# A pre-LN block on one core: first gate and up weights prepared after block 5, LayerNorm rows of chunks 2 and 3 read a column group sooner

## The chip, the cores and the metric

The kernel runs on one NeuronCore of a Trainium2 chip. The metric is the time of one execution on the device, in microseconds (us). TensorE (PE in the profile) multiplies, VectorE (DVE), ScalarE (ACT) and GpSimd (POOL) work on the results, and SyncE (SP) issues most of the DMA transfers.

## The reference

One transformer block on x of 2048 rows and 640 columns, in fp32: sliding-window attention (32 heads of 20 columns, 256 keys back) behind a LayerNorm, then a gated feed-forward (640 to 1536 and back) behind another.

```python
def _A_ref(x, wqkv, wo):
    ...                       # q, k, v of 32 heads, Dh = 20, W = 256
    scores = jnp.einsum("bhqd,bhkd->bhqk", q, k) * (Dh ** -0.5)
    mask = (idx[:, None] - idx[None, :] >= 0) & (idx[:, None] - idx[None, :] < W)
    p = _softmax(jnp.where(mask[None, None], scores, -1e9), axis=-1)
    ...                       # o = p v, heads side by side
    return o @ wo

def _B_ref(x, w_gate, w_up, w_down):
    return (_gelu(x @ w_gate) * (x @ w_up)) @ w_down

h = x + _A_ref(_layernorm(x), wqkv, wo)
h2 = h + _B_ref(_layernorm(h), w_gate, w_up, w_down)
```

## The kernel before

**Number form.** Every fp32 factor is split into two fp16 halves, high and low, after scaling by a power of two. A product takes three matmuls: high by high, high by low, low by high. A weight passes through `Weight`: its raw rows are loaded, `scale` finds the largest magnitude on DVE (the tile `am`) and spreads it over the partitions with one small matmul, `split` writes the high half on ACT, and the low half is written on POOL (the first two pieces of the later weights) or DVE. In the profile the weights are w0 to w2 (q, k, v), w3 (output projection), w4 to w6 (gate, groups 0 to 2), w7 to w9 (up) and w10 to w12 (down); the halves of gate and up of group 0 lie in the tile `gu`. Their raw rows come in slices through a ring of three tiles, `wsl`, once for the maxima and once for the split. The gate, up and down weights behind them come one at a time through a single tile, `wst`.

**Attention.** The 2048 rows are 16 blocks of 128. For each block there are two passes over the scores: one for the row maxima (DVE, the tile `junk`), one for the exponentials (ACT, the tile `pt`). The values are accumulated in the PSUM bank `pv` and copied out by ACT into `oT`, twice per block. When the second half of block j has been copied, `B[j].scored` is set. The output projection adds to x in the tile `ht`, which is stored as rows of h in `h_dram`. `first_norm_lane` normalises blocks 0 to 3 of h from that tile, into a tile of its own, `lxn`, and transposes them with TensorE into `h0h` and `h0l`.

**Feed-forward.** The rows are four chunks of 512, the 1536 columns three groups of 512, each of four tiles (`ft`). `ORDER` lists the pairs (chunk, group). A group of gate and up columns is computed in one of two forms:

- `gate_up`, the plain form: for each tile 30 matmuls of 512 columns into two banks named `mm`. DVE's product of gate and up (the tile `gel`) releases the second.
- `quad`, the form with sums: sums and differences of the two halves of the chunk's rows (`token_sums`, the tiles `ts`) and of the weights (`weight_sums`, the tiles `ws`) replace part of the products. For each tile it takes ten matmuls of 512 columns and 35 of 256, into the banks `tp`, `ra`, `pv` and `rb`, and more additions on DVE and POOL (`quad_out`). The weight sums of a tile take two POOL and two DVE operations; they are stored in DRAM (`wsums`) and read back when a later chunk needs them.

`PLAIN` says how many of the pairs in `ORDER` are plain. In the plain pairs `down` of the pair before runs as a block behind the next one; in the others two of its eight groups of matmuls are laid behind each tile. `norm_start(c)` loads rows of h for chunks 1 to 3 into the ring `wsl`, and `norm_lane` normalises them on DVE and hands them to the DMA transpose on SP (`turned`). Chunk 2 reuses the tiles of chunk 0, and chunk 3 those of chunk 1, so that their transposes may only be issued when gate and up of the old chunk are through.

**Order of the work.** The program is written out by a planner. Each piece of work is a generator, a lane, which yields the engine that it needs next and the condition for it. `Clock` keeps a modelled time for each engine, and at each step the first lane in a list of priorities whose condition holds, and whose engine is not too far ahead (`FFBACK` and its kin), issues one instruction. The order on each engine is thus fixed when the program is built; on the chip each engine takes its instructions strictly in that order and waits for semaphores.

Of the kernel before, what the change touches and what calls it, by code (L numbers as in the profile page):

```python
# [22 lines left out]
P = 128  # L23
# [6 lines left out]
FG = 3  # L30
# [223 lines left out]
def block_kernel(ctx: ExitStack, tc: tile.TileContext, x, wqkv, wo, wg, wu, wd, out):  # L254
# [384 lines left out]
    def hpart(c, b):  # L639
        return tuple(t[:, :, b * P:(b + 1) * P] for t in hT[c])  # L640
# [419 lines left out]
    NCH = S // (CB * P)  # L1060
    ORDER = [(0, 0), (1, 0), (0, 1), (0, 2), (1, 1), (1, 2)]
    ORDER += [(c, fg) for c in range(2, NCH) for fg in range(FG)]
    PLAIN = 4
    hts, ga = {}, {}
    ffpools = [None, None]

# [197 lines left out]
    lnbuf = []  # L1264

    def norm_start(c):
        yield ("sync",), need(when=lambda: pos["gu", c - 2] == FG if c > 1 else (
            ffpools[0] and W["d", 0].ready and all(b.wrote for b in B[CB:2 * CB])), eng="sync")
        if c == 1:
            hT[1] = tuple(nc.tile(ffpools[0], [P, KC, CB * P], F16, n) for n in ("h1h", "h1l"))  # L1270
            lnbuf.extend(nc.tile(stage, [P, D], F32, "wsl", SLICES) for _ in range(3))
        else:
            hT[c] = hT[c - 2]
        for i, n in enumerate("hi"):
            side.append((LATE, norm_lane(c, (i, i + 2), n, lnbuf[i])))

    def norm_lane(c, bs, lane, t):
        for b in bs:
            j = c * CB + b
            yield ("sync",), lambda: nc.others(t, "sync")  # L1280
            nc.sync.dma_start(t, h_dram[j * P:(j + 1) * P, :])
            yield from layernorm(t, lane, *hpart(c, b), xn=lambda: t, dma=True)
            chunk[c] += 1
        if chunk[c] == CB:
            side.append((LATE, token_sums(c)))
# [3 lines left out]
    def token_sums(c):  # L1289
        hh, hl = hT[c]  # L1290
        h1, h2 = hh[:, :, :CW], hh[:, :, CW:]
        l1, l2 = hl[:, :, :CW], hl[:, :, CW:]
        yield on("vector", when=lambda: ffpools[1] and (c == 1 or W["d", FG - 1].ready))
        t = (nc.tile(ffp, [P, KC, 512], F32, "ts") if c % 2 else
             nc.tile(ffpools[0], [P, KC, 512], F32, "wst")).bitcast(F16)
        t = t.rearrange("p c (a n) -> p a c n", a=4)
        for ks in (slice(k, k + 1) for k in range(KC)):
            a, b, m, d = (t[:, i, ks] for i in range(4))
            yield on("vector", h1, h2)
            nc.vector.tensor_tensor(a, h2[:, ks], h1[:, ks], op=ALU.subtract)  # L1300
            yield on("vector", a, l2)
            nc.vector.scalar_tensor_tensor(b, a, -_pow2(-TE), l2[:, ks], op0=ALU.mult, op1=ALU.add)
            yield on("vector", b, l1)
            nc.vector.tensor_tensor(d, l1[:, ks], b, op=ALU.subtract)
            yield on("vector", l2, h2)
            nc.vector.scalar_tensor_tensor(m, l2[:, ks], _pow2(TE), h2[:, ks], op0=ALU.mult,
                                           op1=ALU.subtract)
        TS[c] = t

    WS = {}  # L1310
    QLOAD = [(c, fg) for c in range(2, NCH) for fg in range(FG) if (c, fg) != (2, 0)]
    wsums = dram.tile([FG * FT, P, 4 * KC * P], F16, name="wsums")

    def weight_sums(c, fg, ft):
# [23 lines left out]
    def first_norm_lane():  # L1338

        for b in range(CB):  # L1340
            yield on("vector", when=lambda: B[b].halves == 2)
            yield from layernorm(B[b].h, "h", *hpart(0, b),
                                 xn=lambda: nc.tile(lnp, [P, D], F32, "lxn"))
            B[b].normed = True
            chunk[0] += 1


    later = [(kind, fg) for fg in range(FG) for kind in "gud"]
# [13 lines left out]
    def scale_lane(todo, lane):  # L1362
        for i in todo:
            w = weights[i]
            before = {1: W["q"], 2: W["k"]}.get(i)
            yield on("vector", when=lambda: (w.loaded or w.sliced) and (not before or before.scaled)
                     and (i < NW or B[0].maxima == H) and (i <= NW or B[0].scored))
            yield from w.scale(lane, "ra" if i < NW else "tp")
            if i == 0:
                yield on("vector", sw)  # L1370
                nc.vector.tensor_scalar(qs, sw[:, C_Q:C_Q + 1], _pow2(QE), None, op0=ALU.mult)
                pos["qs"] = 1
            if i == 1:
                yield on("vector", when=lambda: W["q"].known)
                qk_scale()
            if i == NW:
                yield on("vector", when=lambda: W["v"].known)
                wo_scale()
            if i > NW:
                kind, fg = later[i - NW - 1]  # L1380
                if kind == "u":
                    ff_scales(fg)
                    pos["ffk", fg] = 1
                if kind == "d":
                    ff_scales_down(fg)
                    w.down = True
# [81 lines left out]
    def feed_forward():  # L1468
        quads = [(c, fg, ft) for c, fg in ORDER[PLAIN:] for ft in range(FT)]

        def sums_lane():
            for i, q in enumerate(quads):
                yield on("gpsimd", when=lambda: pos["quads"] >= i - 1 and W["d", 2].ready)
                yield from weight_sums(*q)

        side.append((LATE, sums_lane()))
# [167 lines left out]
```

## Time and profile before

| | us |
|---|---|
| median of 3 runs | 1042.01 |
| lowest and highest | 1041.12, 1042.12 |
| the profiled execution | 1043.35 |
| its span, first to last instruction | 1041.6 |

The span divides so: up to about 44 us loads, the first splits and projections; to about 605 us attention, with projections, output projection and feed-forward pair (0, 0) laid between; to 729 us the other plain pairs and their down projections; to the end the pairs with sums.

Times in the profile are us from the span's start, and a mean in a group is in ns. A row of the timeline has start, duration, engine, operation, `out<-in`, and in square brackets how long the engine had idled before and what ended that. "SPq" rows are the issues on SP's queue. All instructions carry line 199, since one helper issues them, so groups are told apart by the names of their tiles.

### The profile page before, as it was taken

How to read it: one execution, taken by the hardware profiler on the slowest of the kernel's cores; microseconds unless marked ns; L12 is line 12 of the kernel's file. 1: busy time of each engine (PE TensorE's matmuls, PEld its weight loads, DVE VectorE, ACT ScalarE, POOL GpSimd, SP SyncE). 2: the span in 40 equal slices, each digit the busy share in tenths (PEclk: the TensorE clock that was granted, in tenths of full speed). 3: DMA queues.
4: the chain of work that ended last, by engine and by line, in shares of the span. 5: the costliest groups of instructions: out<-in, count | busy, mean ns of one | idle time of the engine just before them, and what ended most of it. 6: DMA issues, size and time to landing. Idle time of an engine off the chain costs nothing.

```text
span 1041.6 us, 26895 instructions
## 1 busy us (share of the span) xinstructions
PE 1019.7 (98%) x10802; PEld 691.2 (66%) x10802; DVE 778.4 (75%) x2193; ACT 490.6 (47%) x938; POOL 269.8 (26%) x369
## 2 busy tenths in 40 slices
PE   8999999999999999999999899999999999999998
PEld 7876567667666666676655564555777777777776
DVE  6878989998787777677687867676997985445553
ACT  6512667666666766666667835341122222222220
POOL 7100332233333323232323511031445310000000
PEclk9999999999999999999999999999999999999999
DMA  8663354361341513415302341314342652122211
GB/s 300 149 133 114 119 121 132 122 150 55 73 107 43 101 45 77 77 44 112 129 28 90 78 139 52 101 51 127 102 144 110 164 166 77 59 94 102 77 51 51
DMA packets 89116, 105.86 MB, mean 102 GB/s; under 512 B 22176, under 2 KB 63392, under 8 KB 88992
## 3 DMA queue, kind: packets, MB, share of 16 engines
q1 hardware_dynamic: 76896, 93.41, 31.2%
q10 hardware_dynamic: 12096, 10.75, 3.2%
q8 instruction: 84, 1.38, 0.6%
q14 instruction: 40, 0.33, 0.1%
HBM read 71.11 MB, written 28.84 MB: 96 GB/s over the span
## 4 chain that ended last, share of the span: by engine, by line
PE 78%; DVE 13%; issue 3%; DMA 3%; ACT 2%; POOL 0%; SPq 0%; DVEq 0%; ACTq 0%
PE mm L199 40%; PE pv L199 11%; PE ra L199 11%; PE rb L199 9%; PE tp L199 7%; DVE junk L199 4%; DMA qT<-qk 1%; DVE am L199 1%; DMA wst<-in_wd_dram 1%; DVE m L199 1%; DVE al L199 0%; DVE ht L199 0%; ACT pt L199 0%; DVE qks L199 0%; DMA wsl<-h_dram 0%
## 5 line engine op out<-in xcount | busy, mean ns | idle before, releaser
L199 POOL TENSOR_SCALAR_AFFINE_SELECT pt<-pt 128x512 f32<-128x512 f32 x240 | 152.9, 659 | 361.4 <-ACT pt L199 358.7
L199 DVE CUSTOM_DVE_ANT_0 junk<-rb,mask 128x384 bf16<-128x384 f32 (+2 forms) x262 | 138.9, 530 | 42.4 <-PE rb L199 22.6
L199 DVE CUSTOM_DVE_ANT_0 junk<-ra,mask 128x384 bf16<-128x384 f32 (+2 forms) x250 | 132.2, 529 | 41.4 <-PE ra L199 22.3
L199 ACT ACTIVATE pt<-ra,esc 128x384 f32<-128x384 f32 (+2 forms) x248 | 130.7, 579 | 68.4 <-PE ra L199 57.3
L199 ACT ACTIVATE pt<-rb,esc 128x384 f32<-128x384 f32 (+2 forms) x232 | 122.0, 578 | 70.1 <-PE rb L199 59.2
L199 PE MATMUL pv<-pt,v 128*21 128x128 f32 x2880 | 104.8, 277 | 2.1 <-ACT oT L199 2.1
L199 PEld LDWEIGHTS <-ah 128*128 128x128 f16 x768 | 75.5, 98 | 31.1 <-issue 3.1
L199 ACT ACTIVATE gel<-gel,ffk 128x512 f32<-128x512 f32 x32 | 23.1, 722 | 121.4 <-DVE gel L199 121.4
L199 PEld LDWEIGHTS pv<-pt,v 128*21 128x21 f32 x2880 | 68.8, 101 | 17.0 <-ACT oT L199 2.8
L199 PEld LDWEIGHTS <-kT 62*128 62x128 f16 x1440 | 57.8, 95 | 22.7 <-issue 12.7
L199 PEld LDWEIGHTS <-ws 128*128 128x128 f16 x640 | 62.6, 98 | 7.2
L199 PEld LDWEIGHTS <-gu 128*128 128x128 f16 x440 | 42.1, 98 | 36.6 <-issue 1.5
L199 ACT CAST ah<-gel 128x512 f16<-128x512 f32 x48 | 29.6, 616 | 75.7 <-DVE gel L199 75.7
L199 DVE SCALAR_TENSOR_TENSOR ht<-mm,ffk,ht 128x320 f32<-128x320 f32 x96 | 51.9, 545 | 15.9 <-PE mm L199 13.8
L199 PEld LDWEIGHTS <-qT 60*128 60x128 f16 x640 | 24.5, 93 | 56.7 <-issue 55.3
L199 PE MATMUL mm<-xh,w1h 128*128 128x256 f16 x200 | 54.6, 273 | 1.6 <-DVE qks L199 1.6
L199 PE MATMUL mm<-xl,w1h 128*128 128x256 f16 x200 | 54.7, 273 | 0.0
L199 PE MATMUL mm<-xh,w1l 128*128 128x256 f16 x200 | 54.7, 273 | 0.0
L199 PE MATMUL mm<-w3h,oh 128*128 128x320 f16 x160 | 48.0, 300 | 0.1
L199 PE MATMUL mm<-w2h,xh 128*128 128x320 f16 x160 | 48.1, 300 | 0.0
L199 PE MATMUL mm<-w3l,oh 128*128 128x320 f16 x160 | 48.0, 300 | 0.0
L199 PE MATMUL mm<-w2h,xl 128*128 128x320 f16 x160 | 48.0, 300 | 0.0
(296 smaller groups left out, 2531.8 us busy)
## 6 DMA issues: line engine op xcount, KB each, us to landing
ws<-wsums SPq DMA_DIRECT2D x20, 640.0 KB
qk<-qks ACTq DMA_DIRECT2D x32, 256.0 KB
qT<-qk SPq DMA_DIRECT2D x48, 160.0 KB
kT<-qk SPq DMA_DIRECT2D x48, 160.0 KB
wsums<-ws SPq DMA_DIRECT2D x12, 640.0 KB
ht<-in_x_dram SPq DMA_DIRECT2D x16, 320.0 KB
h_dram<-ht SPq DMA_DIRECT2D x16, 320.0 KB
ht<-h_dram SPq DMA_DIRECT2D x16, 320.0 KB
```

Of the source, the lines that this page charges most:

```text
L199: r = real(*args, **kw)
```

## The change

- `PLAIN` goes from 4 to 3: the pair (0, 2) takes the form with sums, and the down projection of (0, 1) is laid between its matmuls.
- For this chunk 0 gets token sums too, in a tile of its own, `ts0`; the weight sums of a group are built as soon as its gate and up weights are split (before: once the last down weight was), and the rule for which pairs read stored sums is written in general form: those whose group has had sums before.
- `norm_start` for chunks 2 and 3 starts when two of the three groups of chunk c - 2 have been issued (before: all three). The condition on all three moves to the copy ahead of the transpose.
- `scale_lane` starts on the gate weight of group 0, and with it on all weights behind it, when block 5 is scored (before: block 0).
- `first_norm_lane` normalises in place, in `B[b].h`, and starts the token sums of chunk 0 when it is through.

```diff
-    PLAIN = 4
+    PLAIN = 3
...
     def norm_start(c):
-        yield ("sync",), need(when=lambda: pos["gu", c - 2] == FG if c > 1 else (
+        yield ("sync",), need(when=lambda: pos["gu", c - 2] == FG - 1 if c > 1 else (
             ffpools[0] and W["d", 0].ready and all(b.wrote for b in B[CB:2 * CB])), eng="sync")
...
-            yield from layernorm(t, lane, *hpart(c, b), xn=lambda: t, dma=True)
+            yield from layernorm(t, lane, *hpart(c, b), xn=lambda: t, dma=True,
+                                 when=lambda: c < 2 or pos["gu", c - 2] == FG)
...
-        yield on("vector", when=lambda: ffpools[1] and (c == 1 or W["d", FG - 1].ready))
-        t = (nc.tile(ffp, [P, KC, 512], F32, "ts") if c % 2 else
+        yield on("vector", when=lambda: ffpools[1] and (c < 2 or W["d", FG - 1].ready))
+        t = (nc.tile(ffp, [P, KC, 512], F32, "ts" if c else "ts0") if c % 2 or not c else
              nc.tile(ffpools[0], [P, KC, 512], F32, "wst")).bitcast(F16)
...
-    QLOAD = [(c, fg) for c in range(2, NCH) for fg in range(FG) if (c, fg) != (2, 0)]
+    QLOAD = [q for i, q in enumerate(ORDER) if q[1] in [fg for _, fg in ORDER[PLAIN:i]]]
...
             yield from layernorm(B[b].h, "h", *hpart(0, b),
-                                 xn=lambda: nc.tile(lnp, [P, D], F32, "lxn"))
+                                 xn=lambda: B[b].h)
             B[b].normed = True
             chunk[0] += 1
+        side.append((LATE, token_sums(0)))
...
-                     and (i < NW or B[0].maxima == H) and (i <= NW or B[0].scored))
+                     and (i < NW or B[0].maxima == H) and (i <= NW or B[5].scored))
...
-                yield on("gpsimd", when=lambda: pos["quads"] >= i - 1 and W["d", 2].ready)
+                yield on("gpsimd", when=lambda: pos["quads"] >= i - 1 and W["g", q[1]].ready
+                         and W["u", q[1]].ready)
```

## The prediction

> **What bounds the kernel now.** I read the page first, for who is busy; then the table of busy time by stage, with the cuts laid where the order of column groups changes; then the timeline of each engine at the one place where TensorE stands still, and last the groups by line for the prices.
>
> ```profile
> span 1041.6 us, 26895 instructions
> PE 1019.7 (98%) x10802; PEld 691.2 (66%) x10802; DVE 778.4 (75%) x2193; ACT 490.6 (47%) x938; POOL 269.8 (26%) x369
> ```
>
> TensorE is busy for 98% of the span, so only two things can shorten the run: fewer matmuls, or less of the 21.9 us in which it idles and of the time in which its clock is lowered. The stages show where those are (columns: stage, its length, busy time of PE, PEld, DVE, ACT and POOL, granted clock, DMA share, GB/s).
>
> ```profile
> 583.00:586.40 3.40, 1.55 (x31) 1.04 (x32) 2.51 (x4) 1.96 (x4) 1.67 (x2) 1.00 0.35 92
> ...
> 716.29:720.30 4.01, 4.01 (x18) 2.36 (x18) 2.86 (x7) 0.60 (x1) 0.41 (x1) 0.57 0.53 105
> ...
> 115.00:124.40 9.40, 7.66 (x98) 4.15 (x97) 8.82 (x29) 6.81 (x13) 2.44 (x3) 0.92 0.43 128
> 124.40:216.00 91.60, 88.64 (x1216) 59.69 (x1220) 84.98 (x290) 63.12 (x128) 29.61 (x47) 0.99 0.47 128
> ...
> 260.00:340.00 80.00, 79.09 (x1175) 53.91 (x1168) 62.56 (x211) 51.57 (x106) 25.49 (x42) 1.00 0.28 73
> 686.04:712.50 26.46, 26.39 (x124) 11.95 (x122) 17.38 (x25) 9.03 (x13) 9.34 (x6) 1.00 0.27 98
> 712.50:729.38 16.88, 14.88 (x98) 10.07 (x97) 12.82 (x35) 2.79 (x4) 1.65 (x3) 0.90 0.33 79
> 729.38:766.30 36.92, 36.92 (x278) 27.02 (x276) 35.09 (x64) 6.79 (x11) 14.89 (x12) 1.00 0.30 99
> 766.30:803.30 37.00, 37.00 (x279) 27.02 (x277) 30.79 (x55) 8.31 (x14) 17.83 (x13) 1.00 0.38 134
> ```
>
> The row from 686.04 is the plain gate and up of chunk 0, group 2; the row from 712.50 is the down projection of group 1 that stands alone behind it; the row from 729.38 is one whole column group in the form with sums, with eight down groups laid between its matmuls. In that last row TensorE has no gap although DVE is busy for 95%. In the row from 712.50 TensorE loses 2.00 us, and then runs 4.01 us at a clock of 0.57. The timeline names the cause, engine by engine.
>
> ```profile
> 702.68 5.02 SPq L199 DMA_DIRECT2D wsums<-ws  x2
> 705.95 1.40 POOL L199 TENSOR_TENSOR ws<-w5h,ws 128x640 f16<-128x640 f16 x1 [1.36 <-DVE ws L199]
> 707.74 1.38 SPq L199 DMA_DIRECT2D wsl<-h_dram  x2
> 711.95 0.89 DVE L199 BATCH_NORM_STATS2 lsth<-wsl 128x6 f32<-128x320 f32 x2 [3.52 <-DMA wsl<-h_dram]
> 715.50 0.73 DVE L199 SCALAR_TENSOR_TENSOR gel<-mm,ffk,gel 128x512 f32<-128x512 f32 x1
> 715.97 1.23 SPq L199 DMA_TRANSPOSE h0h<-wsl  x1
> 716.29 0.30 PE L199 MATMUL mm<-w11h,ah 128*128 128x320 f16 x1 [2.00 <-DVE gel L199]
> ```
>
> Read it from the bottom. TensorE waits for an mm bank, which the last gelu product (DVE, 715.50) releases. That product stands in DVE's queue behind the row statistics of chunk 2, which waited 3.52 us for rows of h. Those loads were issued at 707.74, because SP had spent 5.02 us on two stores of weight sums, the second of which waited for POOL (705.95 + 1.40 = 707.35).
>
> **The change, part by part.** *Group (0, 2) in the form with sums (PLAIN 3).* The two rows 26.46 + 16.88 = 43.34 us become one stage like the next one, 36.92 us: **-6.4 us**. Of this 2.00 us are the wait, (1 - 0.57) x 4.01 = 1.7 us the lowered clock, and the other 2.7 us fewer matmuls (seven of 256 columns and two of 512 for each k tile in place of six of 512) plus the scale step of the last down weight, whose small matmul stands in the first row; I take 0.5 us of that back, since it only moves: **-5.9 us**.
>
> *Rows of chunks 2 and 3 read a group sooner.* The reads, two rows at first, are then issued when gate and up of (0, 1) have been issued, ahead of the sum stores in SP's queue instead of behind them. Behind the statistics DVE still has the last gelu product of (0, 1) and the accumulations of down (1, 0), and TensorE waits for their mm banks: this is the same configuration at 672. Nothing in SP's queue waits for POOL there, so the rows come 711.95 - 707.74 = 4.2 us after issue, about as the schedule plans them. Cost nothing; if that cover fails, the old 2.0 + 1.7 us return. The transposes now wait for the end of (0, 2); what needs them, chunk 2's first quad, comes two groups later (74 us), and each takes 1.23 us on SP (715.97).
>
> *The first quad needs its weight sums.* This is the added wait.
>
> ```profile
> 680.88 1.40 DVE L199 SCALAR_TENSOR_TENSOR w9l<-wst,sw,w9h 128x512 f16<-128x512 f32 x2
> 686.04 0.38 PE L199 MATMUL mm<-h0h,w6h 128*128 128x512 f16 x1
> 696.38 1.84 POOL L199 TENSOR_TENSOR ws<-w5l,w8l 128x640 f16<-128x640 f16 x1
> 701.25 1.40 POOL L199 TENSOR_TENSOR ws<-w5h,ws 128x640 f16<-128x640 f16 x1 [3.03 <-DVE ws L199]
> 702.61 1.98 POOL L199 TENSOR_TENSOR ws<-w5l,w8l 128x640 f16<-128x640 f16 x1
> ```
>
> The up weight of group 2 (w9) is split by 682.28. A set of sums took 701.25 + 1.40 - 696.38 = 6.3 us the first time and 707.35 - 702.61 = 4.7 us the second: ready at 687.0 to 688.6. TensorE arrives at 686.04, needs the first sum after ten small matmuls and the last one later, so the wait is 0 to about 2 us. All that TensorE does later stands behind it. Later sets have 9.2 us each (36.92 / 4).
>
> *Token sums of chunk 0.* Twenty more DVE operations between the end of attention (605) and 686.
>
> ```profile
> L199 ACT ACTIVATE w5h<-wst,sw x5: 704/706/724, 608.0 to 611.9; 128x512 f16<-128x512 f32 x5
> 627.34 1.23 POOL L199 TENSOR_TENSOR w8l<-wst,w8h 128x512 f16<-128x512 f32 x1 [15.29 <-ACT wst L199]
> 626.93 0.28 DVE L199 TENSOR_TENSOR ts<-h1l,ts 128x256 f16<-128x256 f16 x1
> 627.13 0.42 DVE L199 SCALAR_TENSOR_TENSOR ts<-h1l,h1h 128x256 f16<-128x256 f16 x1
> 627.47 1.25 DVE L199 TENSOR_TENSOR ts<-h1h 128x256 f16<-128x256 f16 x1
> ...
> 605.00:619.20 14.20, 14.18 (x106) 10.14 (x105) 9.37 (x23) 6.65 (x10) 2.31 (x2) 1.00 0.29 101
> 619.20:646.05 26.85, 26.70 (x126) 12.29 (x125) 20.50 (x50) 11.09 (x17) 2.96 (x3) 1.00 0.34 119
> 646.05:672.17 26.12, 26.12 (x123) 12.00 (x122) 17.20 (x31) 11.85 (x19) 4.55 (x4) 1.00 0.31 101
> ```
>
> Ten at 0.28 and ten at 0.42 make 7.0 us; DVE has 4.8 + 6.4 + 8.9 = 20 us idle there, which hides them. Not hidden is a push on the chain of weights (load, maxima, scale, split, then the next load into the one staging tile, five of them from 608 to 682): every push makes w9 later, and the first quad with it. An operation that meets POOL costs more: 1.25 us in place of 0.28, ending 628.72 just after POOL's 628.57. I put push and first wait together at **+1.0 us**, nearer to the low end because the idle time is three times the work; bounds 0 and +9 (below).
>
> [...]
>
> *First gate and up weights after block 5.*
>
> ```profile
> L199 DVE TENSOR_REDUCE am<-wsl 128x1 f32<-128x512 f32 x10 | 6.7, 673 | 0.0
> L199 DVE SCALAR_TENSOR_TENSOR gu<-wsl,sw,gu 128x512 f16<-128x512 f32 x10 | 8.6, 872 | 0.0
> L199 DVE SCALAR_TENSOR_TENSOR gu<-wsl,sw,gu x10: 658/748/1124, 161.4 to 215.2; 128x512 f16<-128x512 f32 x10
> L199 PE MATMUL mm<-h0h,gu x80: 377/379/391, 529.4 to 582.8; 128*128 128x512 f16 x80
> 280.73 0.60 ACT L199 COPY oT<-pv 128x512 f32<-128x512 f32 x1
> ```
>
> 6.7 + 8.6 = 15.3 us of DVE work (with ten ACT copies and the slice loads on SP) leave the stage from 124 to 216 (the last split ends there, 215.2) and come after block 5, whose second half is copied out at 280.73. There is room until the first use at 529.4. DVE falls from 84.98 of 91.60 (93%) to 76%, near the row of 260 to 340 (78%), and that later stretch rises to some 95%. TensorE idles 2.96 us in the first and 0.91 in the other; if they change places nothing is won but part of the clock (0.99). Bounds: -3.4 us (all of the 2.96 and about half a microsecond of clock) and +2.0 (the late stretch pays and the early one keeps its idle time). The idle time before 124.4 lies ahead of the moved work and stays. I take **-0.5 us**, nearer to the middle, since only DVE's load moved.
>
> *Normalising in place, the loads rule, the sums' condition.* The first write in place comes long after the store that must have read the tile:
>
> ```profile
> 145.93 0.34 SPq L199 DMA_DIRECT2D h_dram<-ht  x1
> 156.44 0.60 DVE L199 TENSOR_SCALAR lxn<-ht,lmvh,lyh 128x640 f32<-128x640 f32 x1
> ```
>
> 10.5 us lie between, so it costs nothing; if SP were late by more than that, DVE would stand. Group (1, 2) now loads stored sums in place of building them: four sets are still built for each group, so the count stays at twelve.
>
> **Sum.** -5.9 + 1.0 - 0.5 = -5.4 us on the profiled execution: span 1041.6 to 1036.2. That execution took 1043.35, 1.75 above its span; the median of the three runs is 1042.01, so I move the median by the same 5.4: **1036.6 us**. A difference within 0.2% (2.1 us) can't be told from none here.
>
> **Rivals.** *The stall moves.* The 2.0 us and the lowered clock come back at 672 (statistics) or at 686 (sums), on top of the 1.0: -5.4 + 3.7 = -1.7, 1040.3 us. For it: same order of work at 672. Against: no POOL wait in SP's queue there. Chance 0.14.
>
> *The clock is not the wait's doing.* One row speaks for it:
>
> ```profile
> 585.01 0.85 PE L199 MATMUL pv<-pt,v 128*21 128x128 f32 x24 [1.85 <-ACT oT L199]
> ```
>
> A wait of 1.85 us, in a stage at a clock of 1.00 (583.00 to 586.40). If the stretch at 0.57 had another cause, 1.7 us stay: 1038.3 us. Chance 0.06; against it stands that 0.57 follows the 2.00 us directly. [...]
>
> *DVE becomes the bound in 686 to 797.* Four quads bring about 2.6 us more DVE work each than plain tiles, 10.5 us; today's rows from 686 to 803 hold 17.38 + 12.82 + 35.09 + 30.79 = 96.1 in 117.3 us, then 106.6 in 111. Fully dense it still fits, as 729 to 766 did at 95%; each microsecond over 111 is lost. At 4 to 5 over: 1041 us, no change. Chance 0.10.
>
> *Slower: w9 comes late.* [...] Chance 0.10.
>
> **How the numbers follow.** Forecast 0.60, rivals 0.14, 0.06, 0.10, 0.10. Faster by over 0.2%: the forecast, the clock rival and most of the moved stall, whose time lies near the bound: 0.76. Slower: 0.10; within: 0.14. The range runs from all favourable ends (-5.9 - 3.4 = -9.3) to the no-change rival: 1032.7 to 1041.2, with the slow rival and half of the third outside.
>
> **What would show it.** Right: matmuls with w6 and tp, ra, pv, rb as targets straight behind down (1, 0); one group of 37 us there, no stage at 0.57, and the last quad group ending about 6 us sooner counted from 686; the statistics of chunk 2 on DVE near 676; am on wsl behind 280. Wrong: a PE wait of over 2 us on ws or ts at the first quad, w9l ending after 685, or an idle sum of TensorE in 280 to 380 above 3 us. It all falls if attention ends (605 now) more than 3 us later.

## The result, and the profile after

| | before | after |
|---|---|---|
| median of the runs compared, us | 1042.61 (10 runs) | 1045.47 (10 runs) |
| lowest and highest | 1041.12, 1044.94 | 1044.71, 1050.08 |
| the profiled execution, and its span | 1043.35, 1041.6 | 1044.88, 1042.7 |
| last copy into `oT` (end of attention) | 603.18 | 608.35 |
| from there to the end of the span | 438.4 | 434.35 |

The change makes the kernel slower: the ratio is 1.0031, with a 95% interval of 1.0021 to 1.0041, or +2.86 us, where -5.4 was forecast. The two bottom rows, read from the two profiled executions, say where: what follows the attention is 4.1 us shorter, much as forecast, but the attention ends 5.2 us later. The forecast named that as the point at which all of it falls (more than 3 us).

The page of the changed kernel:

```profile
span 1042.7 us, 27078 instructions
PE 1016.9 (98%) x10862; PEld 696.4 (67%) x10862; DVE 786.1 (75%) x2233; ACT 494.4 (47%) x942; POOL 272.3 (26%) x373
```

TensorE is busy for 2.8 us less than before, and idles for 25.8 us in place of 21.9. The same table of stages as before shows where (stage, length, busy time of PE, PEld, DVE, ACT and POOL, clock, DMA share, GB/s):

```profile
124.40:216.00 91.60, 85.06 (x1150) 56.60 (x1152) 70.75 (x246) 54.06 (x110) 27.54 (x45) 0.95 0.28 74
260.00:340.00 80.00, 78.25 (x1121) 53.67 (x1116) 68.63 (x230) 54.90 (x110) 23.82 (x39) 1.00 0.48 128
...
165.27:170.00 4.73, 4.73 (x23) 2.89 (x24) 1.17 (x3) 1.32 (x3) 1.22 (x2) 0.50 0.02 3
690.06:726.90 36.84, 35.71 (x266) 25.75 (x265) 32.73 (x57) 10.69 (x16) 23.05 (x17) 1.00 0.33 125
```

In the first row DVE has fallen to 77% of the stage, as forecast (76%), yet TensorE is busy 3.6 us less there, not more, and part of the stage runs at half clock. The last row is the pair (0, 2) in its new form. The timelines of TensorE and of SP's queue name the places:

```profile
143.68 0.74 SPq L199 DMA_DIRECT2D kT<-qk  x1
146.51 0.34 SPq L199 DMA_DIRECT2D h_dram<-ht  x1
146.90 4.69 SPq L199 DMA_DIRECT2D kT<-qk  x4
160.49 0.34 SPq L199 DMA_DIRECT2D xt<-in_x_dram  x1
160.88 0.76 SPq L199 DMA_DIRECT2D kT<-qk  x1
...
165.27 0.48 PE L199 MATMUL rb<-kT,qT 60*128 60x384 f16 x1 [5.13 <-DMA kT<-qk]
688.63 0.30 PE L199 MATMUL mm<-w10h,ah 128*128 128x320 f16 x1 [1.03 <-DVE ht L199]
693.49 0.72 PE L199 MATMUL tp<-ts,ws 128*128 128x256 f16 x5 [0.90 <-DVE ws L199]
```

TensorE stands for 5.13 us at 160 to 165 until the last of six transfers has landed that bring the keys of blocks 4 and 5 into the ring `kT` (I call them strips). Five strips were out by 151.6; the sixth was issued at 160.88, right behind a load of x. The clock falls to 0.50 behind the wait. The old stall at 716 and its lowered clock are gone; the waits at the first quad, 1.03 + 0.90 us, are within what the forecast took. In the kernel before the same queue reads:

```profile
146.32 3.14 SPq L199 DMA_DIRECT2D kT<-qk  x4
158.00 0.34 SPq L199 DMA_DIRECT2D xt<-in_x_dram  x1
```

All strips were out by 149.5, and the load of x stood alone behind them.

### The profile page after: what moved, and what is told of

It is laid out like the page before. It is cut to its first block, busy times and chain, and to the rows that moved or that the text cites. A ratio compares the mean times of both kernels' runs of the same rounds, so it can differ in the third digit from the quotient of the medians.

```text
span 1042.7 us, 27078 instructions
## 1 busy us (share of the span) xinstructions
PE 1016.9 (98%) x10862; PEld 696.4 (67%) x10862; DVE 786.1 (75%) x2233; ACT 494.4 (47%) x942; POOL 272.3 (26%) x373
## 4 chain that ended last, share of the span: by engine, by line
PE 81%; DVE 11%; ACT 3%; issue 2%; DMA 2%; POOL 0%; ACTq 0%; SPq 0%; DVEq 0%; POOLq 0%
PE mm L199 39%; PE pv L199 12%; PE ra L199 12%; PE rb L199 10%; PE tp L199 8%; DVE junk L199 2%; ACT pt L199 1%; DVE am L199 1%; DVE ht L199 1%; DMA qk<-qks 0%; DVE gel L199 0%; DVE ws L199 0%; DVE ts L199 0%; DMA wst<-in_wu_dram 0%; DMA kT<-qk 0%
## 5 line engine op out<-in xcount | busy, mean ns | idle before, releaser
L199 POOL TENSOR_SCALAR_AFFINE_SELECT pt<-pt 128x512 f32<-128x512 f32 x240 | 152.5, 657 | 365.5 <-ACT pt L199 365.3
L199 DVE CUSTOM_DVE_ANT_0 junk<-ra,mask 128x384 bf16<-128x384 f32 (+2 forms) x264 | 140.3, 531 | 45.3 <-PE ra L199 25.6
L199 ACT ACTIVATE pt<-rb,esc 128x384 f32<-128x384 f32 (+2 forms) x246 | 130.0, 580 | 75.1 <-PE rb L199 59.7
L199 DVE CUSTOM_DVE_ANT_0 junk<-rb,mask 128x384 bf16<-128x384 f32 (+2 forms) x248 | 131.3, 529 | 42.2 <-PE rb L199 18.4
L199 ACT ACTIVATE pt<-ra,esc 128x384 f32<-128x384 f32 (+2 forms) x234 | 122.4, 576 | 60.5 <-PE ra L199 51.9
L199 PE MATMUL pv<-pt,v 128*21 128x128 f32 x2880 | 104.9, 277 | 2.2 <-ACT oT L199 2.1
L199 PEld LDWEIGHTS <-ah 128*128 128x128 f16 x768 | 75.0, 98 | 28.8 <-issue 1.6
L199 ACT ACTIVATE gel<-gel,ffk 128x512 f32<-128x512 f32 x36 | 26.0, 721 | 139.0 <-DVE gel L199 134.5
L199 PEld LDWEIGHTS pv<-pt,v 128*21 128x21 f32 x2880 | 68.9, 101 | 16.9 <-ACT oT L199 2.8
L199 PEld LDWEIGHTS <-ws 128*128 128x128 f16 x720 | 70.2, 98 | 9.4 <-DVE ws L199 1.2
L199 PEld LDWEIGHTS <-kT 62*128 62x128 f16 x1440 | 58.1, 95 | 21.6 <-issue 11.9
L199 PEld LDWEIGHTS <-gu 128*128 128x128 f16 x440 | 42.0, 98 | 36.7 <-issue 1.4
L199 PEld LDWEIGHTS <-qT 60*128 60x128 f16 x640 | 24.7, 94 | 62.4 <-issue 61.4
L199 ACT CAST ah<-gel 128x512 f16<-128x512 f32 x48 | 29.6, 617 | 70.6 <-DVE gel L199 70.5
L199 DVE SCALAR_TENSOR_TENSOR ht<-mm,ffk,ht 128x320 f32<-128x320 f32 x96 | 52.1, 545 | 11.5 <-PE mm L199 9.5
L199 PE MATMUL mm<-xh,w1h 128*128 128x256 f16 x200 | 54.7, 274 | 1.9 <-DVE qks L199 1.9
L199 PE MATMUL mm<-xl,w1h 128*128 128x256 f16 x200 | 54.7, 273 | 0.0
L199 PE MATMUL mm<-xh,w1l 128*128 128x256 f16 x200 | 54.6, 273 | 0.0
L199 PE MATMUL mm<-w3h,oh 128*128 128x320 f16 x160 | 49.0, 306 | 0.8 <-DVE qks L199 0.8
L199 PE MATMUL mm<-w3h,ol 128*128 128x320 f16 x160 | 49.0, 306 | 0.0
L199 PE MATMUL mm<-w3l,oh 128*128 128x320 f16 x160 | 48.9, 305 | 0.0
L199 PE MATMUL mm<-w2h,xh 128*128 128x320 f16 x160 | 48.1, 301 | 0.0
```

The source lines that it names most:

```text
L199: r = real(*args, **kw)
```

## The experiments

**The parts alone.** First each part of the change was taken away or put in alone. The first kernel is the changed one with `B[0].scored` in place of `B[5].scored`, the second the kernel before with only that delay:

```diff
 # e1_after_block0 (from after)          # e2_before_block5 (from before)
-  ... and (i <= NW or B[5].scored))    -  ... and (i <= NW or B[0].scored))
+  ... and (i <= NW or B[0].scored))    +  ... and (i <= NW or B[5].scored))
```

> The changed kernel with one part undone: gate and up weights of group 0 prepared once block 0 is scored, as before. Theory A (the delay put a load of x ahead of the last kT strip on SP's queue, 5.1 us of TensorE wait and a lowered clock near 165; the feed-forward part gained 4.1 us): attention ends near 603 again, the gain of the feed-forward part stays, about 4 us faster than before, 1038.5. Theory B (the moved DVE work slows the stretch from 281 to 370 and the strip is chance): the same 1038.5, since the work is back. Theory C (the loss comes from normalising in place or from the token sums of chunk 0, not from the delay): stays near 1045.

> The kernel before with the delay alone: first gate and up weights prepared once block 5 is scored. Theory A: TensorE waits about 5 us for a kT strip near 165, attention ends 5 us later, 1047.5 to 1049. Theory B: also later, but without the wait at 165 being the larger part. Theory C: no change, 1042.6.

The third is the first with the rows of LayerNorm read as late as before, so that the form with sums, `ts0` and the normalising in place are left; the fourth is the kernel before with the early rows alone:

```diff
 # e4_plain3_late_norm, on top of e1_after_block0; e5_before_early_rows is the reverse, from before
-  need(when=lambda: pos["gu", c - 2] == FG - 1 if c > 1 else (
+  need(when=lambda: pos["gu", c - 2] == FG if c > 1 else (
```

> The changed kernel with block 0 and with the rows of chunks 2 and 3 read when all three groups are issued, as before; so of the change only group (0, 2) in the form with sums is left, with what it needs. If the form with sums alone removes the old stall at 716 (no plain group ends ahead of the reads any more): equal to the run with block 0 and early rows, about 1038.5. If the early rows are what removes it: the wait of 2.0 us and a lowered clock come back behind the last quad of (0, 2), 1042.

> The kernel before with the early reading of rows for chunks 2 and 3 alone, the plain form kept for (0, 2). If the early rows remove the old stall at 716: 2.0 us and up to 1.7 us of clock less, 1039 to 1040.6. If they only move it to the end of (0, 1), near 672, by DVE statistics and slower weight loads: 1042 to 1044.

| kernel | median, us (range) | ratio to before (95%) | last `oT` copy |
|---|---|---|---|
| e1_after_block0 | 1041.05 (1040.08 to 1043.68) | 0.9983 (0.9973 to 0.9993) | 605.42 |
| e2_before_block5 | 1047.97 (1046.57 to 1050.15) | 1.0046 (1.0032 to 1.0061) | 611.24 |
| e4_plain3_late_norm | 1039.56 (1038.06 to 1041.52) | 0.9966 (0.9953 to 0.9979) | 602.88 |
| e5_before_early_rows | 1041.49 (1039.70 to 1045.37) | 0.9990 (0.9981 to 1.0000) | 605.69 |

The medians of the kernel before beside them were 1042.62 (first three) and 1042.77. So the delay to block 5 costs 5.35 us by itself; the form with sums wins 3.1 us by itself; the early rows, which were forecast at nothing, cost 1.5 us on top of that form (1041.05 - 1039.56), and alone can't be told from no change: in e5 the old stall at 716 is gone, but a wait of 1.09 us for `ht` stands at 686.04. In e4, too, the old stall is gone, so the form with sums removes it without the early rows. Together -3.1 + 1.5 + 5.35 = +3.8 where +2.86 was measured.

**Why the sixth strip is late: the load in front of it?** The first theory was the plainest: the strip is queued behind the load of x, which waits. Three kernels moved one against the other. e3 forbids the planner a load of x between strips. e7 leaves the planner and all other engines alone and exchanges just these two issues on SP. e8 is the mirror in the kernel before: the last strip goes behind the load of x.

```diff
 # e3_after_strips_first: in the lane that loads x
-  yield ("sync",), lambda: max(0.0, nc.slot(att, "xt", 2))
+  yield ("sync",), lambda: INF if pos["strips"] else max(0.0, nc.slot(att, "xt", 2))
 # e7_after_swap_one: planned as before, issued behind the strip
-  nc.sync.dma_start(B[j].x, x[j * P:(j + 1) * P, :])
+  if pos["strips"] and j == 10: held.append(...)      # issued after the last strip
 # e8_before_swap_one: planned as before, issued behind the load of x
-  nc.sync.dma_start(to[rows], ...)
+  if (c, which, par, m) == (2, 1, 1, 2): held.append(...)   # issued after the load
```

> The changed kernel, block 5 kept, but no load of x may be issued between the strips of one qT or kT: the last kT strip of chunk 1 then stands ahead of the x load on SP. Theory A: the wait of 5 us near 165 and the lowered clock behind it go, 6 to 7 us faster than the changed kernel, about 1038.5. Theory B: the wait goes but the time comes back in 281 to 370, about 1044 to 1045.

> The changed kernel with the order of one pair of instructions on SP's queue exchanged, and every other instruction of every engine in the order of the changed kernel: the last kT strip of blocks 4 and 5 is issued ahead of the load of x block 10 instead of behind it. Theory A (this one strip is the loss): the wait of 5.1 us near 165 and half-clock stretches behind it go, 5 to 7 us faster than the changed kernel, 1038.5 to 1040.5. Theory B (the moved DVE work in 281 to 370 is most of the loss; the order planned around it holds the time anyway): the wait at 165 shrinks but the end of attention moves by less than 2 us, 1043.5 to 1045.5.

> The kernel before, with the mirror image: the last kT strip of blocks 4 and 5 issued behind the load of x block 10, all else in its order. Theory A: TensorE waits some 4 to 5 us near 160 for the strip, 1046.5 to 1049. Theory B: the schedule of before has other work at hand there, under 1 us, 1042.6 to 1043.6.

> The changed kernel with the exchanged pair on SP and with the rows of chunks 2 and 3 read late, as before: delay to block 5, group (0, 2) with sums. Theory A with the early rows costing 1.5 us: about 1038 to 1039.5, the level of the run with block 0 and late rows (1039.6). Theory B: near 1043, that level plus most of the 5 us of the delay.

| kernel | median, us (range) | ratio (95%) | TensorE's wait |
|---|---|---|---|
| e3_after_strips_first | 1049.65 (1043.52 to 1054.84) | 1.0062 (1.0041 to 1.0084) | 2.13 us at 161.80, kT |
| e7_after_swap_one | 1046.85 (1044.52 to 1048.63) | 1.0037 (1.0023 to 1.0051) | 5.00 us at 166.21, kT |
| e8_before_swap_one | 1050.32 (1049.88 to 1051.54) | 1.0076 (1.0062 to 1.0089) | 5.51 us at 161.65, kT |
| e9_swap_late_rows (e7 with late rows) | 1044.69 (1043.01 to 1049.45) | 1.0022 (1.0010 to 1.0034) | 4.94 us at 165.44, kT |

e8 shows that the order of one pair of issues is enough to cost 7.5 us. But e7 refutes the theory: with the strip ahead of the load the wait is the same. e3 says little, since its plan changed elsewhere too, and its runs spread over 11 us. e8 itself holds the answer. In its SP queue the load of x went at 150.20, so it held nothing up, and the strip still went at 157.67:

```profile
150.20 0.34 SPq L199 DMA_DIRECT2D xt<-in_x_dram  x1
155.66 1.31 ACTq L199 DMA_DIRECT2D qT<-mT  x2
157.67 0.76 SPq L707 DMA_DIRECT2D kT<-qk  x1
161.65 0.47 PE L199 MATMUL rb<-kT,qT 60*128 60x384 f16 x1 [5.51 <-DMA kT<-qk]
```

The view of what SP's queue waited for (us, times, longest) has, in the same kernel:

```profile
SPq L707 <- DMA qT<-mT: 7.1, 1, 7.1
```

A transfer into `kT` waited 7.1 us for one into `qT`, which ScalarE issued at 155.66 and with which it shares no data. The program as built and the traces explain it. Transfers issued by SP and ScalarE take eight completion semaphores in turn, in the order of the program, and each is issued only when the last transfer on its semaphore, eight places before, has landed (beside what it waits for on its own account). In the trace of the changed kernel the 406 transfers of these two queues carry eight semaphores, and in all 398 pairs that follow each other on one of them the first had landed before the second was issued (before: 402 transfers, 394 pairs). For the changed kernel the list reads:

```
place  transfer                    waits for the landing of
 1     qT<-mT, block 3 (ScalarE)
 2     h_dram<-ht, block 0
 3     kT strip 2
 4     qT<-mT, block 3 (ScalarE)
 5     kT strip 3
 6     qk<-qks, chunk 3 (ScalarE)
 7     kT strip 4
 8     kT strip 5                  kT strip 1
 9     xt, block 10                qT<-mT, block 3   (place 1)
10     kT strip 6                  h_dram<-ht        (place 2)
```

Whoever stands in place 9 waits for the row maxima of block 3. In the kernel before that is a load of x, of block 9, which nobody needs yet; in the changed kernel the load of block 10 with the sixth strip behind it; in e7 and e8 the sixth strip. The view of SP's waits has the row in both kernels: 8.5 us before, where it costs nothing,

```profile
SPq L199 <- DMA qT<-mT: 8.5, 1, 8.5
```

and 8.8 us after:

```profile
SPq L199 <- DMA qT<-mT: 8.8, 1, 8.8
```

In the changed kernel the first qT<-mT of block 3 landed at 160.43, and the load of x, which carries the same semaphore, was issued at 160.49. The wait is on SP's queue, and what is queued behind it waits too: the sixth strip was issued at 160.88, though the store of h in its place 2 had landed at 151.59.

**Moving the wait to where it does no harm.** If that theory holds, it is enough to change who stands in place 9. e10 issues all strips of chunk 2 directly behind the first, e11 is that with late rows. TensorE, VectorE, ScalarE and GpSimd keep the order of the changed kernel.

```diff
 # e10_after_strips_ahead: the other five strips are planned at their places, but issued here
+  if (c, which) == (2, 1):
+      for a, n, k in ((0, 1, 1), (0, 2, 0), (1, 0, 0), (1, 1, 1), (1, 2, 0)):
+          nc.sync.real.dma_start(to[64 * a + DH * n:64 * a + DH * n + DH], strips[a, k])
```

> The changed kernel, with only SyncE's order in the attention touched: the last five kT strips of blocks 4 and 5 are issued right behind the first one, so the store of h rows and the x load of block 10 come after them. All other engines keep the changed kernel's order. Theory (a DMA is let go only when the one eight places before it in the issuing order of SyncE and ScalarE together has landed; in the changed kernel the transfer qT<-mT of block 3 stands eight places before the x load of block 10, and behind that load the last strip is queued; where the load was put behind the strip, the strip itself came onto that place and waited 8 us all the same): the strips are all out by 149 us, the x load takes the wait for qT<-mT instead, as in the kernel before; TensorE's wait of 5.1 us at 165 and the half-clock stretch behind it are gone, the last oT copy comes at 603 to 604 instead of 608.4, and the time is 1041 us (1040 to 1042.5), that of the changed kernel with block zero. Rival (the delay to block five has its cost in the rest of the attention, where TensorE's busy time at 260 to 340 fell from 79.1 to 78.2 us and VectorE's rose): the wait at 165 goes but comes back as others, and the time stays at 1043.5 to 1046. Rival (the strip waits for its own data or for reads of kT): the wait stays at about 5 us and the time at 1045.5.

> The kernel above with LayerNorm's rows of chunks two and three read where the kernel before reads them: delay to block five and the form with weight sums for column group two stay. Theory (the strip is all that the delay to block five costs, and the early rows cost some 1.5 us on top of the sums): 1039.5 us (1038.5 to 1041), like the changed kernel with block zero and late rows (1039.56). Rival (the delay costs by itself): 1042 to 1044.

e10 took 1044.57 us (ratio 1.0015, 1.0004 to 1.0025), e11 1043.43 (1.0006, 0.9998 to 1.0014): 0.9 us less than the changed kernel and 1.3 less than e9, where 4.5 were expected of e10. The wait for the strip was gone, but another of 4.30 us had come, and the clock fell to half again (0.50 at 163.2 to 166.6). The rows of e10, of all three engines:

```profile
156.44 0.45 SPq L199 DMA_DIRECT2D h_dram<-ht  x1
160.49 0.33 SPq L199 DMA_DIRECT2D xt<-in_x_dram  x1
...
160.63 0.61 DVE L199 TENSOR_SCALAR ht<-ht,lmvh,lyh 128x640 f32<-128x640 f32 x1 [4.38 <-DMA h_dram<-ht]
162.38 0.61 DVE L199 TENSOR_SCALAR xt<-xt,lmvx,lyx 128x640 f32<-128x640 f32 x1
...
163.14 1.09 PE L199 MATMUL tp<-ident,xt 128*128 128x128 f32 x4 [4.30 <-DVE xt L199]
```

The load at 160.49 (x of block 10, now in place 9) is not what TensorE waits for. The tile that DVE writes at 162.38 had been loaded long before, since its row statistics ran on DVE at 154; it comes late because DVE stood 4.38 us ahead of `ht<-ht`, the normalising in place of the changed kernel, which may overwrite the rows of h only when their store has read them. e10 moved that store behind the strips, from 146.51 to 156.44, and the strips had themselves waited 5.8 us for a qk transfer (`qk<-qks`) eight places before. In e11 the same wait of DVE is 5.04 us. That a late x of block 10 does no harm here shows in e7 as well: it was issued at 162.35 there, and TensorE has no wait for it up to 175.

The next kernels were planned with the load of x taken for the culprit. Two of them moved both, strip and load, off place 9: e14 in the changed kernel, by issuing the second qT<-mT of block 3 later; e12 in the kernel before with the delay alone, by putting strips and load ahead of the store of h and the second qk transfer of chunk 3 behind the third, so that the store takes the wait. e15 is e14 with the statistics of the early rows late (below).

```diff
 # e14_after_free_loads, on top of e10
-  nc.scalar.dma_start(b.c.qT[...], mT[...])            # both halves
+  if (j, par) == (3, 1): held.append(...)              # issued before the next qk transfer
 # e12_block5_free_loads, on top of e2, with the strips as in e10
-  nc.sync.dma_start(h_dram[j * P:(j + 1) * P, :], b.h)
+  if j == 0: held.append(...)                          # issued behind the load of x, block 10
-  nc.scalar.dma_start(to, both)                        # qk of chunk 3, second
+  if (c, which, ts[0]) == (3, 0, 2): held_qk.append(...)  # issued with the third
```

> The changed kernel as with the strips ahead, and the second transfer qT<-mT of block 3 issued a little later on ScalarE, so that no transfer on which the kT strips or the x load of block 10 depend in the issuing order (eight places before) is late: the strips are all out by 150 us and the x load by 153. TensorE, VectorE and GpSimd keep the changed kernel's order. Theory (the eight-place order is what the delay to block five costs in the attention): TensorE has no wait above 1 us at 155 to 170 (5.1 in the changed kernel for the strip, 4.3 with the strips ahead for the x load), no half-clock stretch there, the last oT copy comes at 602.5 to 604, and the time is 1041 us (1039.5 to 1042), that of the changed kernel with block zero. Rival (the delay costs by itself, and the wait is only where it shows): another wait takes its place, and the time stays at 1043.5 to 1045.5.

> The same for the kernel before with the delay to block five alone (1047.97 us): strips and x load of block 10 ahead of the store of h rows, and the second qk transfer of chunk 3 issued with the third, so that the store takes the wait for qT<-mT. The strips are out by 156 us, the x load at 156.5 in place of 160.5. Theory (eight-place order): no wait above 1 us at 155 to 170, the time falls to that of the kernel before, 1042.5 us (1041 to 1044), where the forecast had the delay at -0.5 (-3.4 to +2.0). Rival (the delay costs by itself): 1045.5 to 1048.

> The first of these with LayerNorm's statistics of chunks two and three begun only at the end of the column group, as in the kernel that had that with block zero (1039.47 us): what the change gives where neither the transfers in the attention nor the statistics before the down weight stand in its way. Theory: 1039.5 us (1038 to 1040.5), so that the delay to block five is worth nothing by itself, plus or minus 1 us. Rival (the delay costs by itself): 1042 to 1044.

e14 missed: 1045.09 us (ratio 1.0019, 1.0010 to 1.0028). The sixth strip now stood eight places behind a qk transfer, which ScalarE had issued at 152.03 and which landed late; the store of h, behind the strips, went at 158.88, and DVE's normalising in place waited for it. SP's waits, and the timeline:

```profile
SPq L782 <- DMA qk<-qks: 6.2, 1, 6.2
```

```profile
158.88 0.44 SPq L199 DMA_DIRECT2D h_dram<-ht  x1
159.43 0.38 SPq L199 DMA_DIRECT2D xt<-in_x_dram  x1
...
162.53 0.61 DVE L199 TENSOR_SCALAR ht<-ht,lmvh,lyh 128x640 f32<-128x640 f32 x1 [6.02 <-DMA h_dram<-ht]
165.04 1.09 PE L199 MATMUL tp<-ident,xt 128*128 128x128 f32 x4 [5.94 <-DVE xt L199]
```

e15 went the same way: DVE waited 4.12 us for the store, TensorE 4.04 us at 162.62, and the time was 1044.66 us (1.0027, 1.0012 to 1.0043). So e10, e11, e14 and e15 say nothing on what the changed kernel would take with strips and store both in time; no run here has that.

e12 starts from the kernel before, which normalises into the tile `lxn` and does not overwrite the rows of h. It worked (timeline, then stages):

```profile
145.52 11.54 SPq L790 DMA_DIRECT2D kT<-qk  x5
157.16 0.45 SPq L944 DMA_DIRECT2D xt<-in_x_dram  x1
162.05 0.34 SPq L944 DMA_DIRECT2D h_dram<-ht  x1
...
156.48 0.61 DVE L199 TENSOR_SCALAR lxn<-ht,lmvh,lyh 128x640 f32<-128x640 f32 x1
159.53 0.63 PE L199 MATMUL tp<-ident,xt 128*128 128x128 f32 x4 [0.39 <-DVE xt L199]
161.36 0.32 PE L199 MATMUL rb<-kT,qT 60*128 60x384 f16 x1 [0.93 <-PE rb L199]
```

```profile
124.40:216.00 91.60, 89.13 (x1245) 60.50 (x1245) 76.73 (x267) 59.36 (x121) 30.24 (x50) 0.98 0.34 82
260.00:340.00 80.00, 77.64 (x1105) 53.01 (x1103) 69.00 (x229) 54.36 (x109) 23.71 (x39) 1.00 0.51 132
```

The strips waited 5.9 us for the qk transfer here too, and were out by 157.06, in time. The wait for `qT<-mT` is on the store, at 162.05, and TensorE's waits there are under 1 us. The attention ends at 604.41, where the same kernel without the moved issues (e2) had 611.24. The time falls from 1047.97 to 1044.45 us (1041.21 to 1047.78; ratio 1.0018, 1.0005 to 1.0031; before beside it 1042.94). So some 3.5 us of the delay's 5.35 are the order of issue, and about 1.5 are left. The profiled execution agrees as far as the attention goes, which ends 1.2 us later than before: TensorE is busy 89.13 us in the first stage, 0.5 more than before (88.64), and 77.64 in the second, 1.45 less than before (79.09). Its time of 1042.75 us is no longer than that of the profiled execution before (1043.35), because the stretch of lowered clock at 716 is missing from it (0.57 before, 1.00 here). Why the second stage loses is not shown; DVE, which has the moved work there, is the candidate.

Two more executions of e12 were profiled, since its runs spread over 6.6 us.

> The kernel with the delay to block five and strips and x load freed, a second execution under the profiler: its first profile has no wait at 160 and ends at 1042.75 us, while the median of its runs is 1044.45. If the same order gives a wait for transfers in other executions (the DMA engines are busy for 0.6 to 0.8 of the time at 140 to 160, so landing times move), this profile shows a wait above 1.5 us for a DMA at 155 to 240 in an execution of 1044 to 1046 us. If it is the lowered clock, it shows more stretches near 0.5 to 0.6 with the same waits.

> The same kernel, a third execution under the profiler. If landing times of the transfers move between executions, its waits at 155 to 240 differ from those of the first two profiles, and its time with them; if the clock moves, the waits are the same and stretches at half clock are not.

They took 1041.69 and 1043.90 us, and their attention ended at 603.00 and 605.72. Both kinds of difference were there. The slower had a wait of 1.36 us for `kT` at 54.98 (0.57 in the other), one of 1.33 at 162.51, and two stretches of lowered clock, at 124 to 128 (0.55 in its first 2 us) and behind 587 (0.65), where the faster had 1.00. Neither had a wait over 2.1 us behind the first 3 us. How the median of 1044.45 comes about beyond these three I leave open.

**The early rows.** In the changed kernel the first statistics of chunk 2 come between the maxima of w9, the up weight of group 2, and its split (VectorE's timeline; the expectation below calls it the down weight). In the last experiment the rows are still read early, but their statistics wait for the end of the group, with block 0:

```profile
678.38 0.15 DVE L199 TENSOR_REDUCE am<-am 128x1 f32<-128x6 f32 x1
678.44 0.48 DVE L199 BATCH_NORM_STATS2 lsth<-wsl 128x6 f32<-128x320 f32 x1
683.40 1.49 DVE L199 TENSOR_SCALAR wsl<-wsl,lmvh,lyh 128x640 f32<-128x640 f32 x1
685.63 1.10 DVE L199 SCALAR_TENSOR_TENSOR lyai<-lyi,lvei 128x1 f32<-128x1 f32 x1 [0.21 <-POOL lyi L199]
688.50 0.73 DVE L199 SCALAR_TENSOR_TENSOR w9l<-wst,sw,w9h 128x512 f16<-128x512 f32 x1
```

```diff
 # e13_block0_rows_early_stats_late, on top of e1_after_block0
             nc.sync.dma_start(t, h_dram[j * P:(j + 1) * P, :])
+            yield on("vector", t, when=lambda: c < 2 or pos["gu", c - 2] == FG)
             yield from layernorm(t, lane, ...
```

> The changed kernel with block zero in place of block five, where LayerNorm's rows of chunks two and three are read a column group early but their statistics on VectorE begin only at the end of that group. It tells apart what the early rows cost (the kernel with block zero: 1041.05 us with them, 1039.56 without). If it is VectorE's statistics, ahead of the conversions of the down weight: the last w9l conversion ends at 682 to 683, TensorE's wait for ht in the first quad falls from 1.09 to under 0.6 us, and the time is 1039.6 us (1038.5 to 1040.5). If it is the two row loads, which share the DMA engines with the load of that weight: the conversion stays at 687 and the time at 1041 us (1040.3 to 1042).

```profile
674.81 0.15 DVE L199 TENSOR_REDUCE am<-am 128x1 f32<-128x6 f32 x1
682.43 1.40 DVE L199 SCALAR_TENSOR_TENSOR w9l<-wst,sw,w9h 128x512 f16<-128x512 f32 x2
...
686.64 0.30 PE L199 MATMUL mm<-w10h,ah 128*128 128x320 f16 x1 [0.50 <-DVE ht L199]
```

It took 1039.47 us (1038.69 to 1039.85; ratio 0.9967, 0.9955 to 0.9979). So the 1.5 us are VectorE's statistics, not the reads: from the end of the maxima (678.53) to the last split (689.23) the changed kernel needs 10.7 us, this one 8.9 (674.96 to 683.83), and the first quad's waits fall from 1.09 + 0.91 us in e1 to 0.50. It was profiled a second time:

> The changed kernel with block zero and the statistics late, a second execution under the profiler, for its spread of only 1.2 us: 1038.5 to 1040, last oT copy at 603.5 to 605, and no wait above 2 us after 60 us.

It took 1039.21 us, beside 1041.48 for the kernel before. e4 and e13 beat both kernels, by 3.0 to 3.1 us against before; they can't be told from each other.

## Why the prediction was wrong

*The step that failed* is "First gate and up weights after block 5", put at -0.5 us with bounds of -3.4 and +2.0; e2 measured +5.35. DVE's load left the early stage as worked out (77%, 76% forecast); in 260 to 340 it rose to 86% only, where the forecast has some 95% (by its own figures, 62.56 + 15.3 of 80 us, 97%). The working took TensorE's idle time in the stage for DVE's doing and asked only whether DVE has room. It did not ask what in the stage is issued earlier when DVE is faster, and what that then waits for: with the delay the planner runs one block of x ahead, the load of x of block 10 comes ahead of strip six, TensorE needs the strip by 160, and the order of issue gave the two the wait for qT<-mT that a load nobody needed had before. The place was there to be read: "SPq L199 <- DMA qT<-mT: 8.5" in the kernel before, a wait for a transfer with which the waiting one shares no data. Freed from that (e12), the delay costs about 1.5 us, within the bounds but at the other end: the early stage won 0.5 us, the late one lost 1.45.

*"Rows of chunks 2 and 3 read a group sooner ... Cost nothing"* was mis-sized: 1.5 us. The cover named there (nothing in SP's queue waits for POOL) held, and the stall did not come back as it was. But the statistics stood on DVE between the maxima and the split of w9, the chain of weights in which, by the forecast itself, every push makes w9 later, and there nobody had counted them.

*The form with sums*, -5.9 + 1.0 = -4.9 us, was right in mechanism: the pair takes 36.84 us against 36.92 forecast, the waits at the first quad were 1.03 + 0.90 us, and from the last `oT` copy to the end the profile is 4.1 us shorter (5.1 in e4: 1036.2 - 602.88 = 433.3). The statistics of chunk 2 stood on DVE at 678, as forecast (676), and no stage of this part has a clock of 0.57. The time of e4 fell by only 3.1 us, and its profiled execution (1038.06) was the fastest of its six; so the term was some 2 us too large for the median. The 1.7 us for the lowered clock would account for nearly all of that: the old stall at 716 stands in the profiles of before, e2, e12 and its two further executions, with waits of 1.81 to 2.00 us, and the clock behind it is 0.57 in the first and 1.00 in the other four. One profile was taken for all executions there.

*Normalising in place and the token sums* cost nothing that could be seen in e4, where the last split of w9 ended at 682.0, as before (682.28). But the condition that the forecast named, a store later by more than 10.5 us, under which DVE would stand, is what the kernels with the strips ahead (e10, e11, e14, e15) ran into: the store went 9.9 to 12.4 us later than after the change (146.51), and DVE stood 4.1 to 6.0 us. The margin was less than 10.5 us, because that was counted to the issue of the store: in e10 4.2 us pass from its issue (156.44) to the write that it held up (160.63).

*The rivals.* None was what happened. The slower rival had w9 late; it was late by 1.8 us in its chain, and the rest by the attention. No run shows the +9 us that bounds push and first wait: the chain's 1.8 us and the first quad's waits of 1.03 + 0.90 us are what was measured, and beside POOL's low parts of w8 (632.41 to 634.93) two operations of the token sums took 1.25 us in place of 0.28 and 1.41 in place of 0.42, 2.0 us more together (1.9 before). The one on the clock, at 0.06, has much for it: the clock was lowered behind such a wait in some executions only (0.65 behind 1.86 us, 1.00 behind 1.85), and at 716 in one of five. The 0.10 for slower came from one mechanism in the feed-forward part, and none stood for the attention, though the text itself said that all falls if it ends 3 us later.

## What to carry to other kernels

When work leaves a busy engine, look not only for where it lands but at what is then needed sooner, and trace the transfers that bring it. A transfer can wait for one with which it shares nothing, if they share a completion semaphore or a queue (here 8.8 us after the change, 7.1 us in e8): read what each queue waits for, and keep a transfer that depends on computed data from standing a ring's length (here eight places) ahead of one that is urgent. Before a store is moved back in its queue, look for the engine that will overwrite the tile it reads. Follow a wait through every engine to the transfer that ended it, and do not stop at the transfer that was issued last. A chain of load, maxima, scale and split should have nothing put between its steps: here statistics between two of them cost 1.5 us.

## What the runs showed of the hardware

Behind a wait of about 2 us TensorE's clock was lowered in some executions and not in others, at the same place in the same program. In the two further executions of e12's program (stage, length, busy times, clock) the faster has:

```profile
585.13:590.00 4.87, 4.64 (x90) 3.21 (x94) 4.17 (x10) 3.18 (x7) 1.25 (x4) 1.00 0.57 135
716.29:720.30 4.01, 4.01 (x30) 2.90 (x30) 3.31 (x10) 0.60 (x1) 0.55 (x1) 1.00 0.55 101
```

and the slower:

```profile
285.57:292.00 6.43, 6.43 (x107) 4.82 (x108) 5.68 (x19) 4.21 (x9) 1.23 (x2) 1.00 0.76 163
587.10:592.00 4.90, 4.90 (x71) 3.42 (x72) 4.20 (x10) 2.52 (x5) 1.29 (x4) 0.65 0.59 134
```

All four stages follow waits of about 2 us (1.85, 1.81, 2.06 and 1.86); one of them lost 0.35 x 4.9 = 1.7 us to the clock. The clock also fell with no such wait: in the slower execution TensorE's longest wait from 117 to 128 is 0.39 us, it is busy for 1.14 of the 2 us from 120, and then

```profile
124.00:126.00 2.00, 1.98 (x28) 1.27 (x27) 1.82 (x8) 1.56 (x4) 1.35 (x2) 0.55 0.21 44
```

where the faster execution has 1.00 in the same stage. Behind the waits over 4 us at 160 to 167 it was lowered each time that a row shows it: 0.50 after the change (165.27 to 170), in e2 (166.6 to 170), e10 and e14 (163.2 to 166.6), 0.61 in e15 (163.2 to 166.6); in e7 and e8 a matmul of 256 columns into mm takes 0.40 and 0.42 us behind the wait, 0.27 ahead of it. So here the clock was lowered behind waits of 1.86 us (0.65) and 2.00 us (0.57, before), and not behind 1.81, 1.85 and 2.06; what decides it, the runs do not show. Where it was lowered behind a wait of about 2 us, it cost about 1.7 us, nearly as much as the 0.2% that a measurement of this kernel can tell; behind the long wait after the change it is more, 0.50 x 4.73 = 2.4 us in the stage from 165.27 alone.
